# Batch 0's third quad of heads attended whole, with the order of all operations written anew

## The chip, the cores and the metric

One core of a Trainium2 chip runs the program. The metric is the device time of one execution in microseconds (us); the figure of the kernel before is the median of three runs. A profile is one further execution, recorded with the start and length of every instruction. Its span runs from the first to the last instruction, and a little more lies around the span.

Six instruction streams matter. PE multiplies matrices, PEld loads their stationary operand, DVE and POOL work element by element, ACT evaluates functions (exp, tanh, square), and SP issues most transfers. Each works through its own list in order; a wait on another engine holds up everything behind it in that list.

## What is computed

Cosine attention over 8 batches, 12 heads, 448 positions and 64 columns, then a highway layer on its output, with 3584 tokens of 768 columns:

```python
q_n = q / (norm(q) + 1e-06); k_n = k / (norm(k) + 1e-06)
scores = q_n @ k_n.T / tau                       # tau = 0.1
x = softmax(scores) @ v                          # then heads are put side by side: 3584 x 768
H = maximum(x @ w_h, 0)
T = 1 / (1 + exp(-(x @ w_t + b_t)))
out = T * H + (1 - T) * x
```

## The kernel before

**Quads and pairs.** The 12 heads of a batch are taken in three quads of four (g = 0, 1, 2) and in six pairs (p = 0 to 5; pairs 2g and 2g+1 belong to quad g). Pair n of the whole program is 6b + p. For a quad, `norm` squares q and k (`sq`) and sums the squares on DVE (`rd2`, line 439, 896 columns, for one quad of q or of k; `rd1` for half of that). The inverse norms come from a logarithm and an exponential on ACT in batch 0 (`ln28`, `ie28`), and from seven Newton steps on DVE in the others (`nt28`, `nt56`, `nt84`). `scale` multiplies by them (`qn7`, `kn7`, line 480, on POOL or DVE), and `turn` transposes the result, on PE with a copy out of PSUM by DVE (`tq`, `tk`, `cpq`, `cpk`, line 499) or by DMA (`xd7`).

**Attention.** A quad that is attended whole has one `tails` and, for each of its two pairs, `scores` and `attend`. `qk n c` makes scores of 448 queries at once, four matmuls on four quarters of the array (line 506); `qkt` does the same for the last 64 keys of the quad's heads. Fourteen ACTIVATEs of 448 columns make the exponentials of a quad (lines 538 and 549). `av n c` (line 566) and `avt n` (line 574) multiply by v and by a column of ones. On DVE `rc` (line 581) takes reciprocals and `ev n` (line 582) scales 448 columns into x.

**The exception.** `WHOLE = 2`: in batch 0 only quads 0 and 1 go that way. Quad 2 is attended by `attend0`, by tiles of 128 queries (i = 0, 1, 2) and one of 64 (i = 3): scores of 128 or 64 columns (`qk01`, `qk02`, `qt01`, `qt02`), exponentials of 384, 512 and 448 columns (line 624), products (`av0`, line 638; `avt0`, line 661), and smaller reciprocals and scalings (`ev0`, line 645; `evt0`, line 666). Each tile completes its own rows of x.

**The highway layer** of a batch has four groups g = 4b + i of rows, three of 128 rows and one of 64. `ffn` needs x transposed: in batch 0 by PE with a copy (`xt6`, then `cpx6`, line 701), in the others by a DMA transpose on SP's queue (`xd6`, line 695). A group has eight products `ff g wi mh lo` of three matmuls on 384 columns (line 715; wi = 0 with w_t, 1 with w_h), a last group four `fft` (line 712) or, at the very end, two `fth` (line 728). They are followed by DVE (`za`, `hm`, `gt`, `gg`), ACT's tanh (`th`), an addition on POOL or DVE (`out`, line 786), and the store. A group of batch b can start once the x it reads is there: the six pairs of its batch, or, in batch 0, the four whole pairs and tile i of quad 2.

**Order.** Nothing is scheduled by the compiler. Operations are numbered in the order in which the text makes them (1842 of them), and `ORDER` lists the numbers in the order of issue; each engine takes its own from that list. `SLOTS` gives the buffer of each tile (PSUM has eight, ring B). `ELSEWHERE` puts single operations on another engine, and `BEHIND` lets an operation wait for one of another engine though no data passes. Before the first data arrive and in gaps of the beginning, PE runs 43 matmuls on zeros (`wm`, `wf`, lines 350 and 354).

**Around the beginning, as listed before.** DVE squares half of quad 0's q (`sq1`, line 433); POOL squares quad 1's q and two quads of batch 1's k (`sq2`, line 431). ACT's list runs through squares and exponentials up to `ex512 2 2 1 1`, the last of quad 2 that the first products wait for. DVE's list reaches `cpx6 1`, the copy of transposed x for group 1, after four `ev`, three `ev0` and eleven `rd2`. PE's first product of the highway layer is `ff 1 0 0 0`; its first of batch 1 is `ff 5 1 0 0`, which needs `ev 11`, the last of batch 1's scalings on DVE, and then `xd6 5`.

Of the kernel before, what the change touches and what calls it, by code (L numbers as in the profile page):

```python
# [90 lines left out]
""".split()  # L91
)
SLOTS = {
    "qr": "01010101",
    "kr": "0120121",
    "kn": "012012012012012201021201",
    "vr": "01010110",
    "vp": "01010101",
    "sq": "012012020102102102102102102020202120210102102012",
    "n2": "01010101",  # L100
    "y": "01201201",
    "tu": "01010101010",
# [789 lines left out]
```

## Time and profile before

| | us |
|---|---|
| median of 3 runs | 247.79 (247.62 to 248.25) |
| the profiled execution | 246.7 |
| its span | 244.9 |
| PE busy | 231.5 |
| DVE busy | 217.4 |
| ACT busy | 206.3 |
| POOL busy | 157.9 |

Busy times overlap, since the engines work side by side. A busy PE is not a PE at its peak: matmuls are pipelined, and the recorded length of one reaches into the next. The start of one against the start of the next is what says how long PE took for it.

### The profile page before, as it was taken

The page shows a single profiled execution, that of the slowest core. Times are in us where ns is not written, and L with a number is a line of the kernel's source. Part 1 is how long each engine was busy: PE and PEld are TensorE (multiplying, and loading weights), DVE is VectorE, ACT ScalarE, POOL GpSimd, SP SyncE. Part 2 cuts the span into 40 slices and gives each one's busy share as a digit, 9 for nine tenths or more (in the row PEclk, how much of TensorE's full clock was granted, in tenths as well). Part 3 has the DMA queues.
Part 4 walks back from the last instruction along what each step waited for, and adds up shares of the span by engine and source line. Part 5 has one row for each costly group of instructions (what it writes and reads, how often), then busy time and mean ns, then how long its engine had stood idle before and what let it go on. Part 6 is the DMA issues. An engine that isn't in the chain of part 4 may idle for free.

```text
span 244.9 us, 8269 instructions
## 1 busy us (share of the span) xinstructions
PE 231.5 (94%) x3304; PEld 143.0 (58%) x3304; DVE 217.4 (89%) x480; ACT 206.3 (84%) x415; POOL 157.9 (64%) x187
## 2 busy tenths in 40 slices
PE   7868899999989999999999999999999999999990
PEld 2334676565765657656664576656565656666550
DVE  4879999999998999999999999899988695768993
ACT  3589999999999999999999999998879787972220
POOL 8596969979983989887676957785665020023340
PEclk9999999999999999999999999999999999999996
DMA  6999999999899969999999899899997647546636
GB/s 224 331 204 265 247 285 225 201 270 226 145 144 235 232 162 230 156 220 220 287 159 202 147 210 212 162 245 197 179 192 156 112 84 148 149 130 130 189 95 155
DMA packets 74647, 47.54 MB, mean 194 GB/s; under 512 B 50288, under 2 KB 71408, under 8 KB 74608
## 3 DMA queue, kind: packets, MB, share of 16 engines
q1 hardware_dynamic: 53776, 32.65, 59.8%
q0 software_dynamic: 19856, 12.68, 39.4%
q10 hardware_dynamic: 976, 1.67, 2.1%
q8 instruction: 26, 0.43, 0.7%
q14 instruction: 13, 0.11, 0.1%
HBM read 38.34 MB, written 11.01 MB: 201 GB/s over the span
## 4 chain that ended last, share of the span: by engine, by line
PE 72%; DVE 10%; ACT 7%; DMA 7%; issue 2%; SPq 1%; DVEq 0%; ACTq 0%
PE B L715 36%; PE B L506 13%; PE B L566 12%; PE B L712 5%; DMA qr<-in_q_dram 4%; ACT E L538 4%; PE B L574 3%; DMA xT<-x 2%; DVE n L439 2%; PE B L496 2%; ACT sq L429 1%; DVE z L744 1%; DVE hm L753 1%; ACT Et L549 1%; DVE qT L499 1%
## 5 line engine op out<-in xcount | busy, mean ns | idle before, releaser
L538 ACT ACTIVATE E<-B 128x448 f16<-128x448 f32 x276 | 135.0, 603 | 9.0 <-PE B L506 6.7
L715 PEld LDWEIGHTS <-xT 128*128 128x128 f16 x576 | 51.2, 98 | 38.7 <-issue 9.6
L786 POOL TENSOR_TENSOR os<-x,hm 128x384 f32<-128x384 f16 x41 | 37.0, 911 | 53.5 <-DVE hm L780 17.4
L715 PE MATMUL B<-wh,xT 128*128 128x384 f16 x288 | 57.2, 326 | 1.0 <-DMA xT<-x 1.0
L715 PE MATMUL B<-wt,xT 128*128 128x384 f16 x288 | 56.3, 326 | 0.1
L439 DVE TENSOR_REDUCE n<-sq 128x14 f32<-128x896 f32 (+1 forms) x50 | 51.0, 1037 | 1.9 <-ACT sq L429 1.7
L506 PE MATMUL B<-qT,kT 64*64 64x448 f16 (+2 forms) x728 | 47.9, 338 | 1.4 <-ACT E L538 0.6
L566 PEld LDWEIGHTS <-E 128*128 128x128 f16 x828 | 38.2, 97 | 10.4 <-issue 5.6
L566 PE MATMUL B<-vp,E 128*128 128x65 f16 x828 | 43.3, 194 | 0.1
L757 ACT ACTIVATE tt<-z 128x768 f16<-128x768 f32 (+1 forms) x32 | 25.9, 810 | 15.5 <-DVE z L744 15.5
L566 PE MATMUL B<-vp,Et 128*128 128x65 f16 x276 | 38.5, 191 | 0.0
L480 POOL TENSOR_TENSOR qn<-qr,y 128x448 f16<-128x448 f32 x38 | 35.0, 935 | 4.5 <-DVE kn L480 1.4
L480 POOL TENSOR_TENSOR kn<-kr,y 128x448 f16<-128x448 f16 x34 | 31.6, 936 | 7.6 <-DVE y L457 2.4
L753 DVE SCALAR_TENSOR_TENSOR hm<-B,x 128x384 f16<-128x384 f32 x53 | 29.0, 551 | 3.9 <-PE B L715 3.5
L744 DVE TENSOR_TENSOR z<-B,bias 128x384 f32<-128x384 f32 x48 | 25.6, 550 | 4.6 <-PE B L715 4.0
L506 PEld LDWEIGHTS <-kT 64*64 64x64 f16 x728 | 17.1, 105 | 20.4 <-issue 15.4
L582 DVE SCALAR_TENSOR_TENSOR x<-B,rd 128x448 f16<-128x448 f32 x46 | 28.0, 617 | 0.7
L566 PEld LDWEIGHTS <-Et 128*128 128x128 f16 x276 | 27.2, 99 | 0.0
L549 ACT ACTIVATE Et<-B 128x448 f16<-128x448 f32 x46 | 26.5, 604 | 0.0
L429 ACT ACTIVATE sq<-qr 128x896 f32<-128x896 f32 (+1 forms) x22 | 22.4, 1018 | 4.6 <-DMA qr<-in_q_dram 4.6
L386 POOL DMA_DIRECT2D vr<-in_v_dram x32 | 22.2, 698 | 5.4 <-DVE vp L511 3.5
L780 DVE TENSOR_TENSOR hm<-tt,hm 128x768 f16<-128x768 f16 (+1 forms) x30 | 15.0, 501 | 0.2
(74 smaller groups left out, 274.4 us busy)
## 6 DMA issues: line engine op xcount, KB each, us to landing
qr<-in_q_dram SPq DMA_DIRECT2D x24, 448.0 KB, 6.8
out_dram<-os SPq DMA_DIRECT2D x47, 192.0 KB, 3.7
kr<-in_k_dram POOLq DMA_DIRECT2D x7, 672.0 KB, 13.8
vr<-in_v_dram POOLq DMA_DIRECT2D x16, 192.0 KB, 10.7
vr<-in_v_dram POOLq DMA_DIRECT2D x16, 144.0 KB, 6.1
out_dram<-os SPq DMA_DIRECT2D x15, 96.0 KB, 3.2
E<-in_k_dram ACTq DMA_DIRECT2D x3, 448.0 KB, 7.5
wt<-in_moe_w_t_dram POOLq DMA_DIRECT2D x1, 1152.0 KB, 23.7
```

The costliest lines, as they stand in the source:

```text
L439: nc.vector.reduce_sum(R("n2", b)[:, c : c + 7 * n], a, axis=AX.X)
L480: ENG[eng].tensor_mul(R(nm + "n", i)[:, :, t, :], source(nm, b, g)[:, t].rearrange("l (j d) -> l j d", d=D), R("y", b)[:, c : c + NJ].unsq ...
L506: nc.tensor.matmul(out[t][64 * h : 64 * h + 64, o[t] : o[t] + w], lhsT=K[ln, j, S_, :], rhs=Q[ln, :, S_, :], start=True, stop=True)
L538: nc.scalar.activation(R("E", n)[:, at : at + 7, :].rearrange("l j x -> l (j x)"), R("B", ("S", n, c, t))[:, 0:S], AF.Exp, scale=1.0 / tau)
L549: op("ACT", f"expt {i} {t}", lambda t=t: nc.scalar.activation(R("Et", (i, t)).rearrange("l j x -> l (j x)"), R("B", ("St", i, t))[:, 0:S], ...
L566: nc.tensor.matmul(U[:, 2 * c + t, :], lhsT=lt.rearrange("l j x -> l (j x)"), rhs=vp[:, 3 * t + m if m < NC else 6 + t, 0:65], start=(m == ...
L582: op("DVE", f"ev {n}", lambda: nc.vector.scalar_tensor_tensor(out=R("x", b)[:, :, D * p : D * p + D], in0=U_()[:, :, 0:D], scalar=0.0, in1 ...
L715: nc.tensor.matmul(P[:, 0:MH], lhsT=xT[:, cc, :], rhs=w_[:, cc, MH * mh : MH * mh + MH], start=(cc == 0), stop=(cc == CC - 1))
L744: op("DVE", f"za {g} {mh}", lambda at=at, sl=sl: nc.vector.tensor_add(R("z", g)[:, sl], R("B", at)[:, 0:MH], biast[:, :] if tail else bias ...
L753: op("DVE", f"hm {g} {mh}", lambda at=at, sl=sl, mh=mh: nc.vector.scalar_tensor_tensor(out=R("hm", g)[:, sl], in0=R("B", at)[:, 0:MH], sca ...
L757: op("ACT", f"th{nb} {g}", lambda: nc.scalar.activation(R("tt", g)[:, 0:W], R("z", g)[:, 0:W], AF.Tanh, scale=0.5), r=[("z", g), ("t0",)], ...
L786: op(e, f"out {g} {mh}", lambda sl=sl, mh=mh, e=e: ENG[e].tensor_add(R("os", g)[:, sl], xpart(mh), R("hm", g)[:, sl]), r=[("gg", g), xk], ...
```

## The change

`WHOLE` becomes 3, so that the loop over `attend0` is empty, and pairs 4 and 5 of batch 0 go through `tails`, `scores` and `attend` like all others. There are 1835 operations in place of 1842. `ORDER`, `SLOTS`, `BEHIND` and `ELSEWHERE` are replaced.

```diff
-    WHOLE = 2
+    WHOLE = 3
...
 ELSEWHERE = {
-    "sq1 q 0 0 0": "DVE",
     "sq1 q 0 0 1": "ACT",
-    "sq2 q 0 1 0": "POOL",
-    "vt 0 1": "DVE",
+    "sq2 k 0 2 0": "POOL",
+    "vc3 0 3 0": "POOL",
...
+    "kn7 0 1 1": "DVE",
+    "qn7 0 2 0": "POOL",
+    "qn7 0 2 1": "DVE",
+    "kn7 0 2 0": "POOL",
     "kn7 0 2 1": "DVE",
-    "sq2 k 1 1 0": "POOL",
-    "sq2 k 1 2 0": "POOL",
+    "sq2 k 1 1 0": "DVE",
+    "sq2 q 1 2 0": "POOL",
+    "sq2 k 1 2 0": "DVE",
+    "qn7 1 0 1": "DVE",
...
```

The entry `vc3 0 3 0` has no effect, since that copy's engine isn't looked up.

Read as names, the new lists of the beginning run so:

- ACT issues all three transfers of k before its table load, squares both halves of quad 0's q and also quad 1's q before `ln28 0 0`, and goes on to `exp 5 0 1`, the last exponential of pair 5: 42 exponentials of 448 columns where 28 stood beside six of 384 and six of 512.
- DVE, from `qn7 0 0 0` on: `qn7 0 0 1; rd2 q 0 1 0; rd2 k 0 1 0; cpq 0 0; cpk 0 0; rd2 q 1 0 0; rd2 q 0 2 0; rd2 k 0 2 0; kn7 0 1 1; qn7 0 1 0; kn7 0 2 1; sq2 k 1 2 0; cpq 0 1; cpk 0 1; ...`. Before `cpx6 1` stand six `ev`, twelve `rd2` and two `sq2`.
- POOL issues the load of w_t before `kn7 0 0 0`, and squares `k 0 2` after `qn7 0 1 1`.
- PE does quad 2's scores and products before `ff 1 0 0 0`, and then takes group 1, group 0 and group 2 among the scores of batch 1. The first product of batch 1 is again `ff 5 1 0 0`; the last scaling that it needs is now `ev 10`.
- At the end the lists are nearly as before: groups 28, 30, 29 and 31, the same last eight products on PE and the same last six instructions on DVE.

More of the change, by code (lines that the diff above doesn't have):

```diff
@@ L95 @@
     "kr": "0120121",
-    "kn": "012012012012012201021201",
-    "vr": "01010110",
+    "kn": "012012012012120210210102",
+    "vr": "01010101",
     "vp": "01010101",
-    "sq": "012012020102102102102102102020202120210102102012",
+    "sq": "012012012010210210201021021021020212012012120012",
     "n2": "01010101",
@@ L102 @@
     "tu": "01010101010",
-    "qn": "012012012120120210012021",
-    "qT": "01230123023132031203123",
-    "kT": "01230123012301231023102",
-    "E": "01230123021032310230121032103210321023103213021032110",
-    "Et": "0123012301230123012301230123012301230123012301",
-    "rd": "01001010101010101010101010101011010101010110101010",
-    "x": "012301230",
-    "xT": "01234510234501325403125403152435",
-    "z": "01010101011001010100010101101010",
-    "tt": "01101010110101001010010110110100",
-    "hm": "01202012022110210210210121110210",
@@ L114 @@
-    "os": "01231212031232013012023230213201",
-    "B": (
-        "0123456701234567012345670123456701234567021356402150202730024016735051743571250757647152674036741563"
-        "0274615327405264301526123750467236547026435147356167035406523745136273405217463234567012405673104765"
-        "2014527451026341567024731652074123067124537523641067352431705642160725407321545361027471642501356072"
-        "4570342163104217054635461023754156473150764137426510654271341325470647235173204165720413250614752405"
-        "4063150473672501437560210147632014260375421672315046315426071562154730146725036127541267054160123572"
-        "6034517036427531026745130613247057264305763240162371042365172403517624"
+    "qn": "012012012120120120120120",
@@ new lines @@
+    "qT": "01230123031203120312031",
+    "kT": "01230123012301201320132",
+    "E": "012301203210321031202130213203123012302312030210310",
+    "Et": "012301230123012302130213021302021302130213021302",
+    "rd": "010010101011010101010101101010101010101010101010",
+    "x": "012301230",
+    "xT": "01234512034152304150324501324512",
+    "z": "01010101010110010100101110001010",
+    "tt": "01101010100101000010101001000100",
+    "hm": "01201021011202102021012021012012",
+    "os": "01231023120101010231320230123010",
@@ new lines @@
+    "B": (
+        "0123456701234567012345670123456701234567103245717415041314530720647407367531027364527653206523104265"
+        "1703426543675142057037156241357061247426301752651427016245134067235604712507643204176543016240571462"
+        "3147260534501623165024705672506725431602513467503612407653265372651724561027340257361062370543507652"
+        "3403624515742063417502421375602376145204723501623740512304621530125734562317026410735432615076134520"
+        "1732750612054736401275017623541732605412360321400527416371460753607524165720634103467630475201436751"
+        "26405370563270531406723465701352710426715463217342603417523067512430"
@@ L134 @@
 ELSEWHERE = {
-    "sq1 q 0 0 0": "DVE",
     "sq1 q 0 0 1": "ACT",
-    "sq2 q 0 1 0": "POOL",
-    "vt 0 1": "DVE",
+    "sq2 k 0 2 0": "POOL",
+    "vc3 0 3 0": "POOL",
     "qn7 0 0 1": "DVE",
     "kn7 0 0 0": "POOL",
-    "qn7 0 1 0": "POOL",
     "kn7 0 1 0": "POOL",
+    "kn7 0 1 1": "DVE",
+    "qn7 0 2 0": "POOL",
+    "qn7 0 2 1": "DVE",
+    "kn7 0 2 0": "POOL",
     "kn7 0 2 1": "DVE",
-    "sq2 k 1 1 0": "POOL",
-    "sq2 k 1 2 0": "POOL",
-    "out 6 1": "DVE",
-    "sq2 k 2 2 0": "POOL",
-    "kn7 2 0 1": "DVE",
-    "out 10 0": "DVE",
-    "vt 3 1": "DVE",
-    "qn7 3 1 0": "DVE",
-    "qn7 3 2 0": "DVE",
-    "kn7 4 0 0": "DVE",
-    "qn7 4 2 1": "DVE",
-    "out 16 0": "DVE",
-    "out 17 1": "DVE",
-    "out 18 1": "DVE",
+    "sq2 k 1 1 0": "DVE",
+    "sq2 q 1 2 0": "POOL",
+    "sq2 k 1 2 0": "DVE",
+    "qn7 1 0 1": "DVE",
+    "out 4 1": "DVE",
+    "sq2 q 2 0 0": "POOL",
+    "kn7 2 1 1": "DVE",
+    "out 10 0": "DVE",
+    "qn7 3 0 0": "DVE",
+    "qn7 3 1 1": "DVE",
+    "out 12 0": "DVE",
+    "out 13 0": "DVE",
+    "out 14 0": "DVE",
+    "out 14 1": "DVE",
+    "vt 4 0": "DVE",
+    "qn7 4 1 1": "DVE",
+    "out 16 1": "DVE",
+    "out 18 0": "DVE",
+    "sq2 q 5 0 0": "POOL",
     "qn7 5 0 0": "DVE",
-    "kn7 5 1 1": "DVE",
-    "out 20 0": "DVE",
-    "out 20 1": "DVE",
+    "kn7 5 0 0": "DVE",
+    "qn7 5 1 0": "DVE",
+    "qn7 5 2 0": "DVE",
     "out 21 1": "DVE",
-    "out 22 1": "DVE",
     "out 23 0": "DVE",
-    "kn7 6 0 0": "DVE",
-    "kn7 6 1 0": "DVE",
-    "qn7 6 2 0": "DVE",
+    "vt 6 0": "DVE",
+    "qn7 6 0 1": "DVE",
+    "out 24 0": "DVE",
     "out 24 1": "DVE",
-    "sq2 q 7 0 0": "POOL",
-    "sq2 k 7 1 0": "POOL",
-    "vt 7 0": "DVE",
-    "qn7 7 0 1": "DVE",
+    "sq2 k 7 0 0": "POOL",
+    "qn7 7 0 0": "DVE",
     "kn7 7 0 0": "DVE",
     "qn7 7 1 1": "DVE",
-    "kn7 7 1 0": "DVE",
-    "kn7 7 1 1": "DVE",
-    "out 29 0": "DVE",
+    "qn7 7 2 0": "DVE",
+    "qn7 7 2 1": "DVE",
+    "out 29 1": "DVE",
 }
```

150 rows, old and new, of tables (BEHIND, ORDER) are left out of this document.

## The prediction

> **What bounds the kernel now.** I read the table of busy time by stage first. Its columns are the stage and its length, then busy time and count of PE, PEld, DVE, ACT and POOL, the granted clock of PE, the DMA share and GB/s.
>
> ```profile
> 10.00:20.00 10.00, 7.19 (x66) 3.27 (x64) 8.26 (x12) 7.90 (x17) 8.62 (x10) 1.00 1.30 237
> 20.00:30.00 10.00, 8.69 (x159) 5.32 (x159) 9.67 (x24) 10.00 (x23) 7.68 (x9) 1.00 1.15 261
> 30.00:40.00 10.00, 9.50 (x210) 7.33 (x211) 9.86 (x27) 10.00 (x21) 8.02 (x11) 1.00 1.15 269
> 70.00:80.00 10.00, 9.04 (x97) 5.56 (x96) 8.70 (x25) 9.42 (x19) 6.17 (x9) 1.00 1.38 189
> 80.00:120.00 40.00, 40.00 (x650) 25.67 (x650) 39.45 (x85) 39.97 (x81) 33.74 (x39) 1.00 1.17 209
> 235.00:245.00 10.00, 3.47 (x45) 2.25 (x43) 5.72 (x15) 0.52 (x1) 0.91 (x1) 0.78 0.56 139
> ```
>
> From 40 us on PE is busy without a break; only 70 to 80 us shows a hole. Up to 40 us PE has holes while ACT and DVE are full. So there are two regimes: a beginning paced by ACT and DVE, and a long stretch paced by PE. DVE is nearly full up to 120 us as well; it is the second bound. The border is the first product of the highway layer, and the hole is in the chain of waits:
>
> ```profile
> 67.96 5.80 DMA xT<-x
> 73.76 0.05 issue
> 73.80 2.61 PE B L715 x15
> ```
>
> The timeline has what lies around it (start, length, instruction):
>
> ```profile
> 38.59 0.65 PE L715 MATMUL B<-wt,xT 128*128 128x384 f16 x3
> ...
> 66.06 1.10 DVE L582 SCALAR_TENSOR_TENSOR x<-B,rd 128x448 f16<-128x448 f32 x2
> 67.08 0.19 DVE L581 RECIPROCAL rd<-B 128x7 f32<-128x7 f32 x1
> 67.31 0.62 DVE L582 SCALAR_TENSOR_TENSOR x<-B,rd 128x448 f16<-128x448 f32 x1
> ...
> 237.31 1.16 PE L728 MATMUL B<-wh,xT 128*64 128x192 f16 x24
> ```
>
> The first product starts at 38.59. The last scaling of batch 1 ends on DVE at 67.93, its transpose lands at 73.76, and PE takes batch 1's first product at 73.80. The last matmul ends at 238.47. The end behind it (DVE, a store) is the same in both kernels, and so I count only what moves that 238.47.
>
> **PE's work.** The unit costs come from the chain as well:
>
> ```profile
> 49.86 0.19 PE B L506 x4
> 50.05 0.59 PE B L715 x3
> 50.64 0.49 PE B L566 x16
> 51.13 0.49 PE B L715 x3
> ```
>
> A score operation (four matmuls) behind another is 0.19; I count 0.20, since some wait a little for a bank. A product of three is 0.49, and 0.59 where the row lies behind a score operation, so a change between the array's forms costs about 0.1. An `av` is 0.49/2 = 0.25. For tiles of 128 queries:
>
> ```profile
> 34.02 0.42 PE L506 MATMUL B<-qT,kT 64*64 64x128 f16 x16
> 34.37 1.18 PE L638 MATMUL B<-vp,E 128*128 128x65 f16 x32
> ```
>
> `qk01` and `qt01` together took 0.35 with a change, so 0.25 for 512 columns on four quarters; that is 0.22 for 448, against 0.20 in one piece. Quad 2's scores go from about 1.5 to seven times 0.20 = 1.4. The change takes out 84 matmuls and 0.1 us. The products with v are as many and as wide before and after.
>
> [...]
>
> Counting the new order of PE by these units: changes of form fall from 183 to 178, fillers left out. More work now stands before the first product (the rest of quad 2, one more transpose of x, one of k). What follows it falls from 195.6 to 194.2: 0.2 of small scores, 0.3 of `avt0`, 0.3 of `xt6` and 0.4 of `tk` move ahead of it, four changes (0.4) go, one `qkt` (0.2) is added. Of that, 33.2 lay before batch 1's first product and 32.2 will; behind it 162.4 and 162.0. In the trace 73.80 - 38.59 = 35.2 for the 33.2, so 2.0 of waits, of which 1.0 are the hole (10.00 - 9.04 in its stage) and 1.0 small ones.
>
> **ACT** has the same 6272 columns of quad 2 in 14 instructions either way.
>
> ```profile
> 15.18 2.69 ACT L538 ACTIVATE E<-B 128x448 f16<-128x448 f32 x6
> 17.72 0.36 ACT L465 ACTIVATE tu<-n,eps 128x28 f32<-128x28 f32 x1
> ...
> 31.60 1.22 ACT L429 ACTIVATE sq<-qr 128x896 f32<-128x896 f32 x1
> 32.44 3.87 ACT L624 ACTIVATE E<-B 128x384 f16<-128x384 f32 x8
> ```
>
> Six of 448 take 17.72 - 15.18 = 2.54, 0.42 each; eight of 384 and 512 take 3.87, 0.48 each, and end at 36.3. Up to the last exponential that the first product needs there were 28 x 0.42 + 12 x 0.48 = 17.5 and will be 42 x 0.42 = 17.8. One square less stands between (32.44 - 31.60 = 0.84), and the square of k of quad 2, which ran before 15.18, is POOL's now, so the exponentials can begin about 0.7 earlier. Against that, the logarithm for quad 2 waits for that square: POOL does it after `qn7 0 1 1`, from some 15.4 on, in 1.7, and DVE's sum takes 1.0. ACT, through with six exponentials at 17.1, would wait for 18.1. I put ACT's end of quad 2 at 36.4, where 36.3 stood. ACT alone moves nothing. That all three transfers of k are issued first costs nothing by my reading: they share one queue, and the fourth load of q on SP's stands before the exponentials in either order.
>
> **DVE** is where the beginning grows.
>
> ```profile
> 8.93 1.86 DVE L480 TENSOR_TENSOR qn<-qr,y 128x448 f16<-128x448 f32 x2 [0.64 <-ACT y L468]
> 10.71 2.07 DVE L439 TENSOR_REDUCE n<-sq 128x14 f32<-128x896 f32 x2
> 12.70 1.34 DVE L499 COPY x<-B 128x896 f16<-128x896 f16 x2
> ...
> 18.80 0.62 DVE L499 COPY qT<-B 128x896 f16<-128x896 f16 x1 [1.42 <-PE B L496]
> ...
> 21.70 0.62 DVE L480 TENSOR_TENSOR kn<-E,y 128x448 f16<-128x448 f32 x1
> 22.24 0.18 DVE L455 SCALAR_TENSOR_TENSOR tu<-tu,n 128x28 f32<-128x28 f32 x1
> ...
> 37.38 0.42 DVE L645 SCALAR_TENSOR_TENSOR x<-B,rd 128x256 f16<-128x256 f32 x1
> 37.72 0.55 DVE L701 COPY xT<-B 128x768 f16<-128x768 f16 x1
> ```
> ```profile
> 5.48 0.62 DVE L433 SCALAR_TENSOR_TENSOR sq<-qr 128x448 f32<-128x448 f32 x1 [1.71 <-DMA qr<-in_q_dram]
> 8.09 1.68 POOL L431 TENSOR_TENSOR sq<-qr 128x896 f32<-128x896 f32 x1 [1.54 <-DMA qr<-in_q_dram]
> ```
>
> `cpx6 1`, the copy that lets the first product start, began at 37.72. Before it the new list has one sum more (12.70 - 10.71 is two, so +1.0), two squares of 896 columns (0.62 for 448, so between 1.0 and 1.24 each, taken as 1.08: +2.2), two scalings of q or k more (22.24 - 21.70 = 0.54: +1.1), two `ev` and two `rc` more (67.08 - 66.06 is two `ev`, 0.51 each, and a reciprocal is put at 0.12 of its 0.19: +1.3), against three `ev0` with their reciprocals (37.72 - 37.38 = 0.34 and 0.1: -1.3) and one copy of v less (0.3). Together +3.9. Against this stand the holes that DVE had: 10.00 - 8.26 = 1.7 in the stage from 10 us, 1.42 of it before the copies of quad 1's transposes, and 0.3 in the next. Of these 2.0 a wait of some 0.8 for POOL's square stays, so 1.2 is recovered. The start is level: `ln28 0 0` now stands behind one more square on ACT (+0.6 or so), but the two `qn7`, which took 1.86 beside POOL's square, have POOL idle beside them and should take 1.1. So `cpx6 1` comes at 37.72 + 3.9 - 1.2 = 40.4 and the first product at about 41.0, 2.4 later than before, with 1.4 us of work less behind it.
>
> From there to the last scaling of batch 1 DVE needed 67.93 - 37.72 = 30.2. By the same units its whole list up to that scaling grows by 2.0 (sum -1.0, squares +2.2, scalings +1.1, `ev` +1.1, small ones of quad 2 -1.2, `rc` -0.2, copies of v +0.2; rounding makes 2.0), and as 3.9 came in early, 1.9 goes out here: 28.3. It ends at 40.4 + 28.3 = 68.7, and with the 5.83 to the landing PE can start batch 1 at 74.5. PE itself arrives at 41.0 + 32.2 + 1.0 = 74.2. So the hole shrinks from 1.0 to 0.3, and batch 1 begins 0.7 later than at 73.80. Behind it stand 162.0 instead of 162.4. **The sum** is +0.7 - 0.4 = +0.3.
>
> Later batches: by my units DVE's list is 4.2 us longer up to the last scaling of batch 2 (two later than for batch 1), and 1.5 to 2.5 up to those of batches 3 to 6. Batch 2 is thus near DVE's limit once more. Each group of 0.5 by which DVE is late there would come on top; I take none and keep 1.0 for the range.
>
> **The time.** The profiled execution took 246.7, 1.1 less than the median of the runs shown; the difference applies to either, so 247.79 + 0.3 = 248.1.
>
> **The rivals.**
>
> *Faster: DVE isn't the pace.* For it: ACT is at 10.00 of 10 from 20 to 40 us, so some of DVE's fullness may be slack in its order, and the new order may place the squares in holes. Then the first product comes at 39.5 (ACT's end at 36.4, then about 1.0 of `av`, 0.65 of `rc` and `ev`, 0.35 of transpose, 0.55 of copy and some queueing), DVE's 28.3 lead from 38.9 to 67.2, and batch 1 starts at 73.0, PE having arrived at 72.7. That is -0.8 - 0.4 = -1.2: 246.6. Against it: DVE's row has 9.67 and 9.86 of 10 in these stages, and 3.9 more must go somewhere.
>
> *Slower: DVE's queue makes the first copy late.* It decides once `cpx6 1` begins after 40.8, since then batch 1 is over 1.1 late and the 0.4 no longer cover it. Every wait that I didn't see in the first 20 us (POOL's square, quad 2's logarithm) shifts DVE one for one, as it has no hole left to catch up in. With 1.4 more, `cpx6 1` is at 41.8, batch 1 at 75.9: +2.1 - 0.4 = +1.7, so 249.5.
>
> *Slower: the array's clock.* In the rows above the granted clock is 1.00 in every stage of the beginning, even with 2.81 of 10 us idle, and 0.78 only in the last, where PE stands still for 6.5. In the new order PE may have little to do for some 3 us before the first product. If the clock fell there for as long again, half a speed would cost 1.5: 249.6. [...]
>
> *The change does nothing:* the 84 matmuls cost 0.1 us of PE, ACT's work is level, and an order as good as the old one gives 247.8. This goes with the forecast.
>
> **How the numbers follow.** About 0.3% (0.74 us) is what a measurement here can tell from no change. The forecast with its neighbour: 0.36. Faster: 0.32. Slower by DVE: 0.27, by the clock: 0.05. The range: the faster case with its own spread of 0.7 below, 245.9; the slower with 0.8 for batch 2, 250.3. These are also what `cpx6 1` between 38.2 and some 42 gives.
>
> **What would show it.** DVE: `cpx6 1` (first line 701) at 40.4, before 39.3 for the faster case, after 40.8 for the slower. First product: 41.0. Last scaling of batch 1: 68.7. Batch 1's first product: 74.5, with a hole of 0.3 before it. ACT: a wait near 17 to 18 us and the end of quad 2 at 36.4. PE: no rows of 64x128, changes of form five fewer, and the last matmul 162.0 + 2.2 behind batch 1's first product (238.47 - 73.80 = 164.7 for 162.4 before). I am wrong if DVE's row shows holes beyond 20 us, if batch 2 or a later one waits for its x by more than 1 us, or if ACT's first exponential comes after 15.2, where it was before.

## The result and the profile after

| | us |
|---|---|
| after, median of 20 runs | 250.19 (248.66 to 253.56) |
| before beside it, median of 20 runs | 247.62 (246.88 to 248.68) |
| ratio | 1.0101, 95% interval 1.0081 to 1.0121 |
| profiled execution after, its span | 249.5, 247.7 |

The change makes the kernel about 1% slower. The time lies inside the range, at its upper end; the forecast itself, no clear change, is wrong. (Here and below a median is that of all runs of a kernel, while a ratio and its interval leave out runs more than 1.5% above the fastest of their kernel, so a ratio can be smaller than the medians suggest.) The table sets the forecast's steps against the trace. Its last column belongs to the experiment `e2_exp_first_warm`, which is told below.

| start, us | before | foretold | after | `e2_exp_first_warm` |
|---|---|---|---|---|
| first exponential | 15.18 | 14.5 | 14.67 | 14.65 |
| last exponential of quad 2 ends | 36.31 | 36.4 | 38.46 | 37.04 |
| `cpx6 1`, copy for the first product | 37.72 | 40.4 | 41.76 | 40.34 |
| first product | 38.59 | 41.0 | 42.46 | 41.04 |
| last scaling of batch 1 ends | 67.93 | 68.7 | 70.10 | 68.61 |
| batch 1's first product | 73.80 | 74.5 | 76.75 | 73.96 |
| last matmul ends | 238.47 | 238.8 | 241.18 | 238.07 |

All that is lost is lost before batch 1's first product: behind it lie 241.18 - 76.75 = 164.4 us, where 164.2 were foretold. It goes in two pieces, against the forecast about 1.4 us up to `cpx6 1` and 0.9 more before batch 1. The table of busy time by stage shows the first (stage and length, busy time of PE, PEld, DVE, ACT and POOL, granted clock of PE, DMA share, GB/s):

```profile
10.00:20.00 10.00, 6.25 (x59) 2.86 (x58) 8.39 (x12) 6.72 (x16) 7.64 (x9) 0.99 1.27 243
20.00:30.00 10.00, 9.35 (x97) 4.49 (x97) 8.63 (x17) 9.15 (x20) 5.32 (x7) 0.67 1.18 271
30.00:40.00 10.00, 9.22 (x206) 6.96 (x207) 9.75 (x30) 9.87 (x21) 5.80 (x8) 1.00 1.16 251
...
70.00:80.00 10.00, 8.77 (x116) 5.19 (x113) 9.18 (x23) 9.95 (x22) 8.75 (x13) 1.00 1.32 190
```

The second row has a clock of 0.67 where before had 1.00. PE looks fuller there than before (9.35 against 8.69), yet it did less: two matmuls on zeros took 1.04 us at half clock (from 24.59) and 0.59 at full (from 26.80), eight matmuls of scores 0.96 (from 22.26) and 0.57 (from 27.32). In steps of 2 us:

```profile
16.00:18.00 2.00, 1.69 (x13) 0.51 (x10) 0.55 (x1) 1.37 (x4) 2.00 (x2) 1.00 1.44 196
18.00:20.00 2.00, 0.63 (x9) 0.60 (x10) 2.00 (x4) 1.43 (x5) 2.00 (x4) 0.96 1.19 262
20.00:22.00 2.00, 1.63 (x9) 0.76 (x8) 2.00 (x4) 2.00 (x5) 1.18 (x2) 0.50 1.16 303
22.00:24.00 2.00, 1.95 (x14) 0.48 (x17) 2.00 (x6) 1.75 (x5) 1.96 (x3) 0.50 1.19 282
24.00:26.00 2.00, 2.00 (x16) 0.87 (x9) 1.69 (x5) 1.67 (x4) 0.15 (x1) 0.50 1.16 284
26.00:28.00 2.00, 2.00 (x29) 1.22 (x26) 0.93 (x2) 1.73 (x5) 0.84 (x2) 0.83 1.27 219
```

Between 18 and 20 us PE works 0.63 of 2, and right behind that the clock is at half. The timeline (start, length, instruction, and in brackets the idle time before it with its releaser) says why PE had nothing to do, and what the half clock cost:

```profile
15.74 1.67 POOL L435 TENSOR_TENSOR sq<-E 128x896 f32<-128x896 f32 x1
...
16.86 0.94 PE L510 MATMUL B<-x 64*64 64x448 f16 x8
...
17.45 1.09 DVE L443 TENSOR_REDUCE n<-sq 128x14 f32<-128x896 f32 x1 [1.49 <-POOL sq L435]
...
18.57 0.32 ACT L469 ACTIVATE tu<-n,eps 128x28 f32<-128x28 f32 x1 [1.21 <-DVE n L443]
...
19.37 0.55 PE L500 MATMUL B<-ident,kn 128*128 128x128 f16 x7 [1.57 <-ACT E L542]
...
26.16 0.80 PE L500 MATMUL B<-ident,kn 128*128 128x128 f16 x7
...
27.07 0.62 DVE L503 COPY kT<-B 128x896 f16<-128x896 f16 x1 [1.37 <-ACT E L542]
...
69.48 0.62 DVE L586 SCALAR_TENSOR_TENSOR x<-B,rd 128x448 f16<-128x448 f32 x1
...
76.75 0.66 PE L719 MATMUL B<-wh,xT 128*128 128x384 f16 x3 [1.24 <-DMA xT<-x]
```

Read from the top it is one chain. POOL squares quad 2's k (`sq2 k 0 2 0`) until 17.4; DVE's sum waits for that and ends at 18.54; ACT's logarithm waits for the sum, 1.21 us, with exponentials queued behind it. Those would empty banks of PSUM. All eight hold scores, so neither the transpose of k nor a filler on zeros can start, and PE stands still for 1.57 us. (The bank comes free at 19.3. The transpose also needs the scaling `kn7 0 1 1`, which stands behind the same sum on DVE and ends at 19.1; experiment 1 shows what that means.) Then the clock is halved for some 6.8 us, reckoned from the rows as (0.04 + 3 x 0.50 + 0.17) x 2 / 0.5, the fillers and scores among it take longer, as above (a single filler 0.61 from 23.16, for 0.38 from 13.14), and the transpose `tk 0 2` comes at 26.16. Its copy on DVE, `cpk 0 2`, waits 1.37 us. (The bracket names ACT, but the copy starts 0.1 after those transposes end, at 26.96.) This is a hole of DVE, in a list that has none to spare. These 1.4 us are what `cpx6 1` is late. The last two rows are the second piece: DVE is through with batch 1 at 70.10, and the DMA transpose lands 6.60 us later, where it took 5.83 before, so that PE waits 1.24.

### The profile page after: what moved, and what is told of

Read it like the earlier page. It is cut to its first block, busy times and chain, and to the rows that moved or that the text cites. A ratio compares the mean times of both kernels' runs of the same rounds, so it can differ in the third digit from the quotient of the medians.

```text
span 247.7 us, 8109 instructions
## 1 busy us (share of the span) xinstructions
PE 233.3 (94%) x3220; PEld 142.6 (58%) x3220; DVE 216.3 (87%) x478; ACT 207.1 (84%) x415; POOL 155.2 (63%) x185
## 5 line engine op out<-in xcount | busy, mean ns | idle before, releaser
L542 ACT ACTIVATE E<-B 128x448 f16<-128x448 f32 x288 | 136.9, 586 | 6.8 <-PE B L510 6.3
L510 PE MATMUL B<-qT,kT 64*64 64x448 f16 x644 | 47.2, 366 | 0.5 <-DVE qT L503 0.2
L570 PEld LDWEIGHTS <-E 128*128 128x128 f16 x864 | 39.4, 97 | 8.9 <-issue 4.8
L484 POOL TENSOR_TENSOR kn<-kr,y 128x448 f16<-128x448 f16 x39 | 36.0, 934 | 9.6 <-DVE tt L763 4.6
L570 PE MATMUL B<-vp,Et 128*128 128x65 f16 x288 | 39.6, 191 | 0.0
L484 POOL TENSOR_TENSOR qn<-qr,y 128x448 f16<-128x448 f32 x32 | 29.6, 934 | 13.1 <-PE B L510 4.2
L586 DVE SCALAR_TENSOR_TENSOR x<-B,rd 128x448 f16<-128x448 f32 x48 | 29.1, 617 | 0.7
L570 PEld LDWEIGHTS <-Et 128*128 128x128 f16 x288 | 28.4, 99 | 0.0
L510 PEld LDWEIGHTS <-kT 64*64 64x64 f16 x644 | 15.5, 105 | 18.3 <-issue 12.5
L433 ACT ACTIVATE sq<-qr 128x896 f32<-128x896 f32 (+1 forms) x22 | 20.9, 953 | 4.6 <-DMA qr<-in_q_dram 4.6
L390 POOL DMA_DIRECT2D vr<-in_v_dram x32 | 22.2, 695 | 1.5 <-POOLq L877 0.8
```

The source lines that it names most:

```text
L484: ENG[eng].tensor_mul(R(nm + "n", i)[:, :, t, :], source(nm, b, g)[:, t].rearrange("l (j d) -> l j d", d=D), R("y", b)[:, c : c + NJ].unsq ...
L510: nc.tensor.matmul(out[t][64 * h : 64 * h + 64, o[t] : o[t] + w], lhsT=K[ln, j, S_, :], rhs=Q[ln, :, S_, :], start=True, stop=True)
L542: nc.scalar.activation(R("E", n)[:, at : at + 7, :].rearrange("l j x -> l (j x)"), R("B", ("S", n, c, t))[:, 0:S], AF.Exp, scale=1.0 / tau)
L570: nc.tensor.matmul(U[:, 2 * c + t, :], lhsT=lt.rearrange("l j x -> l (j x)"), rhs=vp[:, 3 * t + m if m < NC else 6 + t, 0:65], start=(m == ...
L586: op("DVE", f"ev {n}", lambda: nc.vector.scalar_tensor_tensor(out=R("x", b)[:, :, D * p : D * p + D], in0=U_()[:, :, 0:D], scalar=0.0, in1 ...
```

## The experiments

The theory: the half clock is the loss, and without it the forecast's working holds. The rivals are that DVE's longer list is worth more than was reckoned, clock or not, or that the transfers before batch 1 are the loss. (Where an expectation below gives its theories letters, the letters are its own.)

**1. The hole filled.** Two kernels move three exponentials ahead of the logarithm on ACT, so that banks come free; the second also puts six matmuls on zeros into PE's hole.

```diff
 ACT
-... expt 0 1; ln28 0 56; exp 1 0 1; ie28 0 56; exp 1 2 1; sq2 k 1 0 0; exp 0 0 0
+... expt 0 1; exp 1 0 1; exp 1 2 1; exp 0 0 0; ln28 0 56; ie28 0 56; sq2 k 1 0 0
 PE (e2_exp_first_warm only)
-... qk 0 0; tk 0 1
+... qk 0 0; wg 0; wg 1; wg 2; wg 3; wg 4; wg 5; tk 0 1
```

> The changed kernel with three exponentials of pairs 0 and 1 moved ahead of the logarithm for quad 2 on ACT, which fills ACT's wait near 17.4 us; PE's hole of 17.4 to 19.4 us stays. Theory (the clock): the granted clock is still 0.50 from about 20 to 26 us, DVE still waits about 1.4 before the copy of k of quad 2, the first copy of transposed x comes at 41.3 to 41.8, and the median is 249.5 to 250.2. Rival (ACT's wait is what came late): the first copy comes near 40.7 and the median is about 249.1.

> As the kernel with the exponentials moved ahead, and with six matmuls on zeros more, in PE's hole between 17.8 and 19.1 us. Theory (the clock): the granted clock stays at 1.00 from 20 to 28 us, DVE's wait before the copy of k of quad 2 is gone, the first copy of transposed x comes at 40.2 to 40.6, the median is 248.4 to 249.0, and the runs spread by no more than those of the kernel before. Rival (DVE's longer list alone): the clock doesn't matter, and the median is that of the kernel without the six matmuls, 249.5 to 250.2.

Measured: `e1_exp_first` 251.24, ratio 1.0081 (1.0040 to 1.0121); `e2_exp_first_warm` 247.34, ratio 0.9992 (0.9967 to 1.0018). Stages of the second, in the same columns:

```profile
18.00:20.00 2.00, 2.00 (x20) 1.16 (x19) 2.00 (x4) 1.97 (x6) 2.00 (x4) 1.00 1.19 264
20.00:22.00 2.00, 0.80 (x6) 0.14 (x3) 2.00 (x4) 2.00 (x5) 1.17 (x2) 1.00 1.16 304
...
70.00:80.00 10.00, 10.00 (x118) 5.75 (x117) 9.96 (x26) 10.00 (x22) 8.83 (x13) 1.00 1.12 196
```

Its timeline at `cpx6 1` and at the end of batch 1:

```profile
40.34 1.48 DVE L709 COPY xT<-B 128x768 f16<-128x768 f16 x3
...
67.99 0.62 DVE L590 SCALAR_TENSOR_TENSOR x<-B,rd 128x448 f16<-128x448 f32 x1
...
73.96 0.66 PE L723 MATMUL B<-wh,xT 128*128 128x384 f16 x3
```

Six matmuls that compute nothing, the only difference between the two kernels, take the whole 1% away, where a median of 248.4 to 249.0 was expected. The clock stays at 1.00, `cpx6 1` starts at 40.34, where 40.4 was foretold, batch 1's scalings end at 68.61 (68.7), and no hole is left at 70 to 80 us.

The moved exponentials alone give nothing. The first kernel is even slower than both theories had it: in its profile the half clock lasts 10.2 us and `cpx6 1` comes at 42.39. Its lines on DVE and PE say why free banks don't close PE's hole:

```profile
18.51 0.62 DVE L484 TENSOR_TENSOR kn<-E,y 128x448 f16<-128x448 f32 x1
```
```profile
19.28 0.91 PE L500 MATMUL B<-ident,kn 128*128 128x128 f16 x7 [1.42 <-ACT y L472]
```

The transpose `tk 0 1` can't start before this scaling, `kn7 0 1 1`, has ended at 19.13, and the scaling is next on DVE behind the sum that waits for POOL's square. So the late square holds PE in two ways, by the banks and by DVE's list. The exponentials free the banks, which is of use only where a filler stands ready for them, as in the second kernel.

The first kernel also shows where the second piece grows: its wait before batch 1's first product is 2.5 us, and a second half clock follows it.

```profile
70.00:80.00 10.00, 7.55 (x104) 4.32 (x101) 9.12 (x22) 10.00 (x23) 8.74 (x12) 0.99 1.34 140
80.00:90.00 10.00, 10.00 (x126) 5.74 (x125) 7.01 (x13) 5.95 (x12) 5.18 (x7) 0.84 1.07 211
```

**2. Holes in the kernel before.** Seven of its fillers are taken out. PE then stands still for 0.97, 0.72 and 0.76 us between 12 and 16 us, where it was 0.97, 0.29 and 0.71.

```diff
-    for i in range(NF):
+    for i in (0, 2, 4, 5, 10):
```

> The kernel before without seven of its matmuls on zeros, those between 13 and 23 us. Theory (the clock): one stage between 14 and 27 us shows a granted clock near 0.5, and the time rises by 0.5 to 2 us, to 248.2 to 249.7, with a wider spread. If no stage shows a lower clock, the time stays at 247.6 and the run says only that these holes are too short. Rival (the fillers do nothing): the clock drops and the time stays at 247.6.

Measured: 247.67, ratio 1.0006 (0.9984 to 1.0028).

```profile
16.00:18.00 2.00, 1.86 (x11) 0.65 (x11) 1.58 (x2) 2.00 (x6) 2.00 (x3) 0.70 1.43 195
18.00:20.00 2.00, 1.96 (x18) 1.31 (x16) 1.07 (x2) 2.00 (x7) 1.97 (x2) 0.50 1.35 214
...
24.00:26.00 2.00, 2.00 (x35) 1.56 (x30) 2.00 (x7) 2.00 (x7) 1.05 (x2) 0.50 1.20 231
26.00:28.00 2.00, 2.00 (x39) 1.71 (x37) 0.94 (x3) 1.57 (x4) 2.00 (x3) 0.74 1.13 243
```

A miss for "a half clock costs its time". Here it lasts 10.2 us, longer than in the kernel after, and `cpx6 1` is only 0.88 later (38.60 for 37.72); the median doesn't move by more than 0.7 us. The old order loses less where the clock falls: the same 10.2 us make `cpx6 1` 2.0 later in the new one (experiment 4). Why the median doesn't show even the 0.88 stays open. In the profiled execution the last matmul is 1.5 later, but that execution took 248.6, above its median, and the one of before 246.7, below its own; I don't build on it.

**3. The old order with quad 2 whole.** `WHOLE = 3` in the kernel before, with quad 2's operations put by hand where those of the tiles stood.

```diff
-    WHOLE = 2
+    WHOLE = 3
...
-qk01 2 0 0; ex384 2 0 0 1; qk01 2 1 1; ...
+qk 4 0; exp 4 0 0; qk 4 1; ...
```

> The third quad attended whole, but in the order of the kernel before: its operations stand where those of the tiles of 128 queries stood, with two exponentials more ahead of the first product; DVE's squares and scalings are as before. Theory (DVE's longer list and the clock, both from the new order): DVE's list up to the first copy of transposed x is level, the copy comes at 39.0 to 39.5, behind the two exponentials, the clock stays at 1.00, and the median is 247.3 to 248.2. Rival (attending the quad whole is what costs): the first copy comes after 40.5 and the median is 249.3 or more.

Measured: 251.57, ratio 1.0181 (1.0131 to 1.0230). The clock is 1.00 from 10 to 40 us, but `cpx6 1` starts at 40.79: quad 2's last exponential ends at 37.56 and its scaling only at 40.2, because I put other work of PE ahead of the last products with v. Then PE waits 2.64 us before batch 1, and the clock falls behind that (0.93 and 0.90 in the stages from 70 and 80 us). That is what the rival expected, but by my reading it comes from where I put that work. It shows that `cpx6 1` can be late with quad 2 whole and no half clock; it doesn't price the change apart from its order.

**4. Other traffic before batch 1.** One load of 672 KB of k stands about 4 us ahead of the transposes on POOL. It brings batch 4's k. Four kernels exchange it with the load of batch 5's k, which then comes behind them. (The expectations here and in experiment 5 call these loads those of quads; a load is that of a whole batch.)

```diff
 POOL
-... ldk 5 0 (near 45 to 50 us) ... ldv3 3 1 0; ldk 4 0; ... out 1 1; ...
+... ldk 4 0 (near 45 to 50 us) ... ldv3 3 1 0; ... out 1 1; ldk 5 0; ...
```

> The kernel after, with two loads of K exchanged on POOL (quad 4's takes the place of quad 5's near 45 us, quad 5's is issued behind out 1 1, near 73.5 us), so that no 672 KB load lies in front of the DMA transposes that feed batch 1's first product. Theory A, only the clock's dip at 20-27 us costs: the wait of 1.32 us before ff 5 1 0 0 goes (landing 6.6 -> 4.5-5.5 us), and the time follows by no more than that, 249.0 us (248.7 to 249.4), the windows 20:26 still at 0.50. Theory B, in most executions the late chain brings a second dip behind that wait: the median falls by more than the profiled wait, to 248.0 us or less. Theory C, the landing isn't set by the load in front: 250.2 us, landing still 6.2 us or more.

> e1_exp_first with the same exchange of loads. The hole of PE at 17.8-19.1 us and the first dip (20 to 28 us at 0.50) stay. Theory B (wait for the transpose, then a second dip at 80-90 us): the landing falls from 7.8 to 5.0-5.5 us, the wait of 2.54 us before ff 5 1 0 0 falls under 0.5, the window 80:90 returns to 1.00 and the median to 247.8 us (247.3 to 249.0). Theory A (the first dip is the whole cost): 250 us or more and 80:90 at 1.00 or not without a change of the time.

> e2_exp_first_warm with the same exchange of loads: neither the early hole of PE nor the load in front of the transposes. If both causes are named rightly the median is 246.6 us (246.2 to 247.3), its runs lie within 1.5 us of each other instead of 3, no window of the profile behind 10 us is under 0.95, and it stands 0.2 to 0.6 per cent under the kernel before. If the exchange does nothing where there is no wait: 247.3 us.

> The kernel before with the same exchange (quad 5's load behind out 1 0). Its wait of 1.14 us before ff 5 1 0 0 goes with the landing of 5.83 us falling to about 4.7. If that wait sets the end: 246.6 us (246.2 to 247.0), ratio 0.996. If the wait is hidden by what follows: 247.7 us. This says whether the two orders differ beyond the two holes: by e7's expectation and this one they end level, 246.6 us both.

Measured: 253.38, 253.12, 251.21 and 248.56, ratios 1.0202, 1.0146, 1.0132 and 1.0063 (intervals from 1.0142 to 1.0261, 1.0096 to 1.0197, 1.0075 to 1.0188, 1.0035 to 1.0090). All four are slower, against all that was expected. The expected part did happen: the first transpose lands 4.5, 4.5, 4.0 and 2.9 us after the last scaling, and batch 1 starts without a wait (73.89 in the third, 74.73 in the first). But now the transposes of batch 3's q come late. The wait of the third between 84 and 96 us, and the stage behind:

```profile
PE B L514 <- DMA qT<-qn: 2.7, 1, 2.7
```
```profile
90.00:100.00 10.00, 7.77 (x72) 3.90 (x73) 6.28 (x11) 6.38 (x13) 6.69 (x7) 0.83 1.12 324
```

PE waits 2.7 us for a transpose of q (2.3 and 2.4 in the first two), and a half clock of 3.4 us follows in all three. In the fourth no half clock is seen and no wait is over 0.6 us. So the load in front does weigh on the landing, but in the first three its removal only moves the wait to 89 us, where it costs more. That the moved load is what holds the transposes of q is my reading; no run tests it.

One thing these runs show by chance. Up to 40 us the lists of `e5_loads_apart` are those of the kernel after, and those of `e6_exp_first_loads` are those of `e1_exp_first`. Yet the half clock lasted 3.4 us in the one and 6.8 in the other, and none in the one and 10.2 in the other. `cpx6 1` started at 40.36 with none, 41.20 with 3.4, 41.76 with 6.8 and 42.39 with 10.2. That is the price of the half clock up to there: 0.8, 1.4 and 2.0 us. (The kernels with none and with 10.2 have the three exponentials moved, the others not.) `e6_exp_first_loads` has PE's hole of 1.42 us and no filler, and its `cpx6 1` comes as in `e2_exp_first_warm`. So it is the half clock that delays `cpx6 1`, and not the hole by itself.

**5. The squares.** Three kernels: the two squares that the change gave to DVE back on POOL; the square that makes ACT wait back on ACT; and, for the spread of the runs, the load of k 2.4 us sooner.

```diff
 ELSEWHERE (e9_squares_pool, on e2_exp_first_warm)
-    "sq2 k 1 1 0": "DVE",
-    "sq2 k 1 2 0": "DVE",
+    "sq2 k 1 1 0": "POOL",
+    "sq2 k 1 2 0": "POOL",
...
 ELSEWHERE (e10_square_act, on the kernel after)
-    "sq2 k 0 2 0": "POOL",
+    "sq2 k 0 2 0": "ACT",
...
 POOL (e11_warm_k_early, on e2_exp_first_warm)
-kn7 2 0 1; qn7 2 1 0; kn7 2 2 0; qn7 2 2 0; kn7 2 2 1; ldv3 3 1 0; ldk 4 0
+kn7 2 0 1; kn7 2 2 0; kn7 2 2 1; ldk 4 0; qn7 2 1 0; qn7 2 2 0; ldv3 3 1 0
```

> e2_exp_first_warm with the two squares that the change gave to DVE (sq2 k 1 2 0 and sq2 k 1 1 0, 1.08 us each) back on POOL, behind kn7 0 2 0 and qn7 0 2 0, and quad 3's load of K behind them. If DVE's list is what sets cpx6 1 once the clock stays up, cpx6 1 starts at 38.7 to 39.3 us instead of 40.34 (2.16 us less of DVE, held back by the last exp of quad 2, which can't end before 36.3), the first product near 39.7 and the median is 246.1 us (245.7 to 246.7). If DVE has slack there (its summands reordered), nothing moves: 247.3 us. If POOL, now later with vt 0 1 and vt 0 0, holds the first av: 248 us or more, with rc 0 later than 30.9.

> The kernel after with one engine changed back: the square sq2 k 0 2 0 on ACT as before the change (placed ahead of sq2 q 0 2 0, where ACT is idle at 12-13 us) instead of POOL. If the hole of PE comes from ACT's wait for this square (POOL 15.74 to 17.4, its sum 17.45 to 18.45), ln28 0 56 stands at 17.2 to 17.5 instead of 18.57, no window of 2 us between 18 and 28 is under 0.9 of the clock, cpx6 1 starts by 40.3 and the median is 247.3 us; with the sum rd2 k 0 2 0 now at 15.9 instead of 17.45 DVE's list can be up to 1.5 us earlier still: cpx6 1 at 38.9 and 246.0 us. If the hole has another cause (all banks full whatever the square does), the dip stays: 250 us.

> e2_exp_first_warm with quad 4's load of K 2.4 us sooner on POOL (kn7 2 2 0 and kn7 2 2 1 ahead of qn7 2 1 0; the load near 62.2 instead of 64.57), all later loads where they were. If the load in front of the transposes spreads the runs (246.4 to 249.4 in e2): 246.8 us median and a spread of 1.5 us. If not: 247.3 us, the same spread.

Measured: 250.34, ratio 1.0123 (1.0087 to 1.0159); 250.08, ratio 1.0080 (1.0044 to 1.0117); 249.38, ratio 1.0085 (1.0053 to 1.0117).

The first is a miss for a reason that no theory had. Its timeline on DVE and POOL:

```profile
22.26 3.49 DVE L519 COPY vp<-vr 128x576 f16<-128x576 f16 x1
```
```profile
21.30 1.70 POOL L439 TENSOR_TENSOR sq<-kr 128x896 f32<-128x896 f16 x1
22.94 0.95 POOL L488 TENSOR_TENSOR qn<-qr,y 128x448 f16<-128x448 f32 x1
23.84 1.69 POOL L439 TENSOR_TENSOR sq<-kr 128x896 f32<-128x896 f16 x1
```

A copy of v that takes DVE 0.34 in the kernel after takes 3.49 here, and it ends at 25.75, when POOL's three instructions have ended at 25.53. Everything behind it is late, PE does nothing from 24 to 26 us, the clock falls for 3.4 us, and `cpx6 1` starts at 43.30. The worth of the two squares on DVE was therefore not measured. That POOL's instructions are what held the copy is read from these times alone, and by what means they held it no run shows.

The second has what its first expectation said: the logarithm stands at 17.55 and `cpx6 1` at 40.27, with no filler added.

```profile
18.00:20.00 2.00, 1.24 (x17) 0.95 (x15) 1.64 (x3) 2.00 (x6) 1.18 (x2) 1.00 1.22 250
20.00:22.00 2.00, 1.51 (x11) 0.34 (x10) 2.00 (x4) 2.00 (x6) 1.74 (x2) 1.00 1.16 296
```

So most of the hole does come from the square that the change moved to POOL: 0.72 us of it are left, before 20.21. The further gain on DVE's list doesn't come: ACT waits 0.7 us for a load of q before it squares `q 1 1`, and DVE's sum of that square starts at 28.77, where it was 28.89 in `e2_exp_first_warm`. But the median stays at 250.08. Its twelve runs fall in two groups: five with a mean clock under 0.99 have a median of 252.40, seven with 0.99 or more 249.05. So in some executions the clock seems to fall still; the profiled one (0.994) isn't among them, and where it falls in the others no run shows. What the second group has against `e2_exp_first_warm`, 1.7 us, fits waits for transposes of x; the profile has 1.3 before batch 1 and 0.8 at 160 us, and `e2_exp_first_warm` none.

The third cost itself a wait of 2.0 us (PE for `qn7 2 1 0`, which now comes later on POOL) and says nothing on the spread. Its load is out of the transposes' way, and the first lands after 4.5 us.

**6. Both cures.** The square on ACT, and three fillers in the hole that was left, with `exp 0 0 0` moved so that a bank is free.

```diff
 ACT
-exp 1 2 1; sq2 k 1 0 0; exp 0 0 0
+exp 1 2 1; exp 0 0 0; sq2 k 1 0 0
 PE
-tk 0 1; tq 0 1; wf 4
+tk 0 1; tq 0 1; wg 0; wg 1; wg 2; wf 4
```

> e10_square_act with exp 0 0 0 ahead of the square sq2 k 1 0 0 on ACT, so that a bank of PSUM comes free at about 19.2 us, and three matmuls of zeros (wg) behind tq 0 1, in the hole of PE that e10 still has at 19.5 to 20.2 us. Nothing behind 21 us is changed. If e10's median (250.08, single runs from 247.3 to 253.8 with clocks from 0.979 to 0.997) comes from that hole, which brings the dip in some executions and not in others, the median is 247.4 us (247.0 to 248.2), every single clock is 0.990 or more and the spread under 3.5 us. If it comes from the transposes of x (waits of 1.44 us before ff 5 1 0 0 and 0.99 before ff 18 0 1 0 in e10's profile), which this doesn't touch, it stays at 249 to 250.5 us with a spread of 5 us or more.

Measured: 248.09, ratio 1.0022 (1.0005 to 1.0039), runs from 246.63 to 250.55 with clocks from 0.987 to 0.998.

```profile
18.00:20.00 2.00, 1.89 (x18) 1.25 (x18) 1.79 (x3) 2.00 (x6) 0.92 (x3) 1.00 1.20 263
```

0.65 us of work more for PE, with the exponential moved, go with a median 2.0 us lower than before; by the ratios it is 0.6%, or 1.4 us. The median is as expected; three clocks are under the 0.990 that was expected of all, and the runs spread by 3.9 us instead of under 3.5. By the ratios 0.3%, some 0.7 us, remain against `e2_exp_first_warm`; the profile has PE wait 0.8 for the transpose before batch 1, and 0.7 (for a bank that DVE empties) near 159 us. No version that I ran beats the kernel before.

## Why the prediction was off

**The step that failed** is that of DVE's holes: "a wait of some 0.8 for POOL's square stays, so 1.2 is recovered". The wait was seen, and rightly put on ACT and DVE, though too small: 18.1 was foretold for the logarithm's start and it is 18.57, and DVE waits 1.49 for the square. It wasn't followed to PE: ACT's wait keeps the banks full, DVE's wait holds the scaling that the next transpose needs, and PE stands still for 1.57 us. The half clock behind this is the term that the sum didn't have: 1.4 us at `cpx6 1`. With it falls the sentence that the clock stayed at 1.00 "even with 2.81 of 10 us idle", which I took for safety. The 2.81 was several holes of up to 0.97 us; 18 to 20 us is a single one of 1.57, with 0.63 of 2 busy.

The clock rival had the right mechanism and nearly the right time (249.6), but at another place, just before the first product, and with a chance of 0.05 that is far too small. That its time is so near is luck: it had nothing for the wait before batch 1. The range holds the measured time, in part by luck too. The DVE rival's numbers came nearly out (with 1.4 more, `cpx6 1` at 41.8; it is 41.76), and DVE did shift one for one, but it waited for a transpose that the half clock made late, and not for a wait of the first 20 us. The 0.8 that the range adds for batch 2 happens to cover batch 1's transpose, which landed 0.8 later. The clock rival's half speed is what the rows show (0.50), but its some 3 us of idleness were my estimate, and no run shows that so much is needed: in the trace the clock fell behind a hole of 1.57 us, with 1.69 of 2 us busy just before, and for 6.8 us.

**The other steps**, by the table. DVE's list: with the clock up `cpx6 1` is at 40.34 against 40.4 foretold, and from there to the last scaling of batch 1 it takes 28.27 (28.3 foretold; 28.34 in the kernel after). The second sum stands. The first is right by two errors that cancel. From DVE's first pair of sums on (10.71 and 10.60) its holes up to `cpx6 1` are 2.21 us before and 2.07 in `e2_exp_first_warm`, where the wait for POOL's square alone is 1.50: 0.1 is recovered, not 1.2. Its work grows from 24.8 to 27.7, by 2.9, not 3.9; the Newton steps, which the sum leaves out, take 0.5 less, and the rest is spread over its terms. That it is DVE's list alone that sets 40.3 isn't shown: in `e10_square_act` the list gets past the sum for quad 2's k 1.5 earlier, and a load of q holds it to the same time. ACT: the wait near 17 to 18 us is there, the first exponential comes at 14.67, quad 2 ends at 37.04 instead of 36.4 (38.46 with the half clock). (42 x 0.42 is 17.6, not 17.8; neither is what set that end.) PE: 164.4 behind batch 1's first product for 164.2.

**Mis-sized** is the landing of the transposes. I took 5.83 as a constant. From the last scaling to the landing of the first transpose it was 4.81, 6.20, 6.60, 6.71 and 7.82 us in the profiles of `e2_exp_first_warm`, `e12_square_act_warm`, after, `e10_square_act` and `e1_exp_first`, with the same load in front. In every profile with that load some 4 us in front the transpose lands only behind it: 0.6 to 0.9 us behind the load's own landing in before, `e2_exp_first_warm`, `e3_before_cold`, `e9_squares_pool` and `e12_square_act_warm`, and 2.2 to 2.3 in after, `e1_exp_first`, `e4_old_order_whole` and `e10_square_act`. So what was to be forecast is the landing of the load (74.41 in the kernel after, 72.78 in `e2_exp_first_warm`).

Of the signs by which I would be wrong one appeared: DVE's holes beyond 20 us. Batch 2 and the later ones didn't wait for x by more than 1 us.

**What stays open.** In the profiles the kernel after loses 241.18 - 238.07 = 3.1 us against `e2_exp_first_warm`: 1.4 by the half clock up to `cpx6 1`, 1.4 from there to batch 1's first product (1.24 of it the wait for the transpose), 0.3 spread behind. Why that transpose lands now 0.6 and now 2.3 us behind the load in front of it isn't settled, since the lists of these kernels are the same there. Nor is it shown how much of the second piece the medians contain, since each kernel has one profile. For the half clock there is more: the mean granted clock was 0.973 to 0.989 in the twenty executions of the kernel after, and 0.991 to 0.996 in the twelve of `e2_exp_first_warm`.

## To carry to other kernels

When a change adds a wait on one engine, follow it to the banks that this engine would have emptied and to the operands that stand behind the same wait, and from there to PE: here a wait of 1.21 us on ACT became a hole of 1.57 in PE, a half clock of 6.8 and, with the late transfer behind it, 1% of the kernel. Look for the clock's risk in stages as short as 2 us, since one of 10 hides the hole, and judge a kernel near the edge by many runs, since here the same lists had 10.2 us of half clock in one profile and none in another. A gap that can't be closed can be filled with matmuls on zeros, if a bank is free for them: six of them, 1.46 us, went with a clock of 1.00 in `e2_exp_first_warm`.

## What the runs showed of the hardware

- The half clock came in lengths of 3.4 us (`e5_loads_apart`, `e9_squares_pool`, `e4_old_order_whole`, and the second one of `e1_exp_first`), 6.8 (after) and 10.2 (`e1_exp_first`, `e3_before_cold`): once, twice and three times the same. I reckon them from the granted clock as in the first section. Why the lengths stand in these steps no run shows.
- Holes of PE behind which the clock fell were 1.42 us (`e1_exp_first`), 1.57 (after), 2.3 to 2.7 (waits for transposes), and 2.8 (`e9_squares_pool`); in `e3_before_cold` it fell behind three of 0.97, 0.72 and 0.76 between 12 and 16 us. It stayed at 1.00 with a hole of 1.42 us from 20.8 to 22.2 us in `e2_exp_first_warm`, and in `e6_exp_first_loads` with the very hole of `e1_exp_first` (PE busy for 0.79 of the 2 us from 18). So no length of a hole separates the two here.
- A copy of v on DVE took 0.34 us in the kernel after (from 23.12, with only the issue of a load on POOL beside it) and 3.49 in `e9_squares_pool` (from 22.26), beside three instructions of POOL that followed one another until 25.53; it ended at 25.75, and not between two of them.
